# A transformer block with sliding attention: small LayerNorm operations on ScalarE, a wait for GpSimd's power, attention weights turned by VectorE

## The chip, the core and the metric

The kernel runs on one core of a Trainium2 chip. A core has five engines with their own instruction lists: TensorE (PE in the profile) multiplies matrices into PSUM, VectorE (DVE) and ScalarE (ACT) do elementwise work, GpSimd (POOL) small general work, and SyncE (SP) issues DMAs. They run side by side and wait for each other on semaphores only. The metric is the device time of one execution in microseconds. Before the change the median of three runs is 239.69 us (237.97 to 240.04).

## What is computed

One block with a residual stream `x` of 2048 positions by 512 features, in bf16. It has adaptive LayerNorm (shift, scale and gate come from a condition vector `c`), attention of 32 heads of 16 features over a window of 8 positions that lie 2 apart, and a gated feed-forward part with 1792 hidden features.

```python
mod = (silu(c) @ w_mod).reshape(1, 6, 1, -1)
sa, ca, ga, sb, cb, gb = mod[:, 0], mod[:, 1], mod[:, 2], mod[:, 3], mod[:, 4], mod[:, 5]
h = layernorm(x) * (1 + ca) + sa
# attention: H, W, dil = 32, 8, 2
idx = arange(S)[:, None] - (arange(W) * dil)[None, :]      # the 8 positions of each query
logits = einsum('bhsd,bhswd->bhsw', q, k[idx]) * 16 ** -0.5
logits = where(idx >= 0, logits, -1e9)
o = einsum('bhsw,bhswd->bhsd', softmax(logits), v[idx])
x = x + ga * (o @ wo)
h = layernorm(x) * (1 + cb) + sb
x = x + gb * ((silu(h @ w1) * (h @ w3)) @ w2)
```

## The kernel before, in words

Positions are cut into 16 tiles of 128 (`T` = 0 to 15). The program first records operations (`Program.op`, `Program.dma`), each with its engine, its function and what it reads and writes. Then `place` puts them in the order of a written-out table `ORDER`, and buffers in the slots of a table `SLOTS`. Each engine runs its operations in the order in which the table has them, and no other. `synchronize` adds the waits that follow from reads and writes and from the reuse of buffers (`o.prev`). So a list is fixed, and an engine whose next operation isn't ready stands still, even if a later one is.

The stages, and the lines that the prediction names:

- Lead: 24 warm-up matmuls on a constant (`warm`, L518), the modulation from `c` (L504), loads on SyncE (`load_x`, L413; all DMAs are issued at L124). Tiles 0 and 1 come in one load.
- First LayerNorm (`ln_stats`): VectorE statistics (L555, L556), plus epsilon (L561 on VectorE for tiles 0 and 1, L563 on GpSimd after), the power -0.5 on GpSimd (L565), then the normalisation on VectorE (L571 for tile 0, L576 for the others). `ln_T` turns the result on TensorE (L636) or by DMA, and ScalarE or VectorE scales and shifts it (L644, L651, L621).
- Projections of q, k (L691) and v (L711). v goes out to DRAM and comes back shifted (`values`), eight positions side by side on the partitions.
- `logits`: VectorE multiplies q with the eight shifted k in one operation of 4096 elements (L742, the large product `sb_pq`), and TensorE sums over each head with 32-column matmuls, four side by side (L752). For tile 0 one more matmul (L749) puts the mask in.
- `shift`, `exps`, `softmax`, always for a pair of tiles: maximum (L764), subtraction (L769), exponential on ScalarE (L782), sum (L794), reciprocal (L796), product (L797). Then `turn`: TensorE transposes the weights, four transposes of 128x128 for a pair (L807), and ScalarE copies them out of PSUM (L811).
- `values`: VectorE multiplies the shifted v with the weights (L827, 4096 elements, the value product), TensorE sums them (L855), ScalarE copies (L861), a DMA transposes, TensorE multiplies with `wo` (L867), and VectorE adds the residual (L871).
- Second LayerNorm (`ln_sums`), for a pair of tiles: mean on GpSimd (L586), squares on ScalarE (L590), variance plus epsilon (L596), power (L597) and bias (L599) on GpSimd, normalisation on ScalarE (L601).
- Feed-forward part: `ffn_unit` has two matmul groups (L883), a silu on ScalarE (L889) and a product on VectorE (L892); `ffn_w2` multiplies with w2 (L921, L909) and `store` adds the residual (L931) and writes out.

The table interleaves the feed-forward part of early tiles with the attention of later ones. `o.lock` marks operations that hold a port which VectorE and GpSimd share: by default those of GpSimd, and by hand the large VectorE operations (L576, L742, L827, the scaling of `wo` and `w2`). Before the change nothing in the program reads that mark.

Of the kernel before, what the change touches and what calls it, by code (L numbers as in the profile page):

```python
# [73 lines left out]
class Program:  # L74
# [68 lines left out]
    def place(self, order, slots):  # L143
# [129 lines left out]
def _build(p, A_x, A_wqkv, A_wo, B_w1, B_w3, B_w2, c, w_mod, out):  # L273
# [36 lines left out]
    before = sb([P, W, 2, 16], bf, "before")  # L310
# [114 lines left out]
    load_x(0, 2, 1)  # L425
# [123 lines left out]
    def ln_stats(Ts):  # L549
# [10 lines left out]
        if i < 2:  # L560
            o = p.op("dve", lambda e: e.tensor_scalar(rsn, mv[:, i:i + n, 1], EPS, None, op0=ALU.add), 65, k, r=vms, w=[va])  # L561
# [6 lines left out]
        for T in Ts:  # L568
            vn = Val("xn", xnpool)
            if T == 0:  # L570
                p.op("dve", lambda e, vn=vn, T=T: e.scalar_tensor_tensor(vn.at[:], x_sb[:, T, :], mv[:, T, 0:1], bass.AP(rs, T, [[2 * NT, P], [0, D]]),  # L571
                                                                         op0=ALU.subtract, op1=ALU.mult), 600, ("nm", T),
                     r=[vx[T], vr] + vms, w=[vn])
                vns.append(vn)
                continue
# [6 lines left out]
    def ln_sums(Ts):  # L582
# [3 lines left out]
        p.op("pool", lambda e: e.tensor_scalar(nm[:, i:i + n, 0], sx[:, i:i + n, 0], -1.0 / D, None, op0=ALU.mult), 215, k,  # L586
             r=[vsx[T] for T in Ts], w=[vnm])
        for T, vn in zip(Ts, vns):
# [7 lines left out]
        o = p.op("pool", lambda e: e.tensor_scalar(rsn, var[:, i:i + n, 0], 1.0 / D, EPS, op0=ALU.mult, op1=ALU.add), 210, k, r=vvs, w=[va])  # L596
        o = p.op("pool", lambda e: e.tensor_tensor(rsn, rsn, bass.AP(cst, 1, [[2, P], [0, n]]), ALU.pow), 600, k, r=[va, vcst],  # L597
                 w=[vr], lead=o)
        p.op("pool", lambda e: e.tensor_tensor(nb[:, i:i + n, 0], nm[:, i:i + n, 0], rsn, ALU.mult), 210, k, r=[vr, vnm], w=[vb], lead=o)  # L599
        for T, vn in zip(Ts, vns):  # L600
            p.op("act", lambda e, vn=vn, T=T: e.activation(vn.at[:], x_sb[:, T, :], ACT.Identity, bias=nb[:, T, :],  # L601
# [129 lines left out]
    def logits(Ts):  # L731

        vl = Val("ps_l", psum)
        for i, T in enumerate(Ts):
# [11 lines left out]
            def red(e, i=i, T=T, vp=vp):  # L746
                c0 = vl.at * 512 + i * W * 32
                if T == 0:
                    e.matmul(PALL[0:32, c0:c0 + W * 32], ones[:, 0:32], before[:], start=True, stop=False, tile_position=(0, 0))  # L749
                for ft in range(KT):  # L750
                    for q in range(4):
                        ins = e.matmul(PALL[32 * q:32 * q + 32, c0:c0 + W * 32], E_sb[:, ft, :], bass.AP(vp.at, ft * P + 32 * q, [[W * KT * P, P], [KT * P, W], [1, 2], [2, 16]]),  # L752
                                       start=(ft == 0 and (T > 0 or q > 0)), stop=(ft == KT - 1), tile_position=(0, 32 * q))
# [35 lines left out]
    def softmax(Ts, vl, ve, vx_):  # L789
# [7 lines left out]
        p.op("dve", lambda e: e.tensor_tensor(ve.at[0][:, 0:n], bass.AP(PALL, bank(vl).offset, [[8 * 512, P], [W * 32, n], [1, 32], [32, W]]),  # L797
# [279 lines left out]
```

## Time and profile before

| | |
|---|---|
| median of three runs (lowest, highest) | 239.69 us (237.97, 240.04) |
| span of the profiled execution | 237.7 us |
| instructions in it | 4535 |
| HBM read, written | 29.62 MB, 4.21 MB |
| GpSimd: L596, L597, L599 of the second LayerNorm, mean of eight | 766, 703, 618 ns |
| GpSimd: L563, L565 of the first, mean of seven | 207, 706 ns |
| ScalarE's L590 and L601 | 714 and 806 ns |

The profile is of one execution, and its span runs from the first to the last instruction of the core. A "busy" time is a sum over one engine. A row of the timeline has start, length, engine, line, operation, output and inputs with partitions by elements, and a count where several are merged; instructions of one engine overlap a little, so several in a row take less than the sum of their lengths. In square brackets stands how long the engine had been idle, and what ended it. A row of the waits reads: who waited, for whom, microseconds in all, how often, the longest. A row of the stretches has, for each engine, busy time and instructions in that stretch, then TensorE's granted clock, the DMA engines' busy share and the rate. "PEld" is TensorE's loading of weights, which runs beside its matmuls.

### The profile page before, as it was taken

The page shows a single profiled execution, that of the slowest core. Times are in us where ns is not written, and L with a number is a line of the kernel's source. Part 1 is how long each engine was busy: PE and PEld are TensorE (multiplying, and loading weights), DVE is VectorE, ACT ScalarE, POOL GpSimd, SP SyncE. Part 2 cuts the span into 40 slices and gives each one's busy share as a digit, 9 for nine tenths or more (in the row PEclk, how much of TensorE's full clock was granted, in tenths as well). Part 3 has the DMA queues.
Part 4 walks back from the last instruction along what each step waited for, and adds up shares of the span by engine and source line. Part 5 has one row for each costly group of instructions (what it writes and reads, how often), then busy time and mean ns, then how long its engine had stood idle before and what let it go on. Part 6 is the DMA issues. An engine that isn't in the chain of part 4 may idle for free.

```text
span 237.7 us, 4535 instructions
## 1 busy us (share of the span) xinstructions
PE 229.7 (97%) x1781; PEld 136.2 (57%) x1806; DVE 179.4 (75%) x279; ACT 138.5 (58%) x267; POOL 29.2 (12%) x66
## 2 busy tenths in 40 slices
PE   7999999999999998999999999999999999999995
PEld 4776454445588674664444444444475457485774
DVE  5699999999999989999999999682654403434433
ACT  2289577999978744985865594837473405040300
POOL 4434100013002000240002520012010000000000
PEclk9999999999999999999999999999999999999999
DMA  6999999999999999897981693642203000000202
GB/s 216 372 337 322 158 237 299 208 269 283 353 200 270 243 249 199 173 260 177 247 234 47 182 234 72 154 132 46 67 19 91 3 0 0 6 19 0 70 0 88
DMA packets 46317, 38.85 MB, mean 163 GB/s; under 512 B 21704, under 2 KB 37080, under 8 KB 46296
## 3 DMA queue, kind: packets, MB, share of 16 engines
q1 hardware_dynamic: 46288, 38.56, 66.9%
q8 instruction: 14, 0.23, 0.4%
q14 instruction: 7, 0.06, 0.1%
q10 hardware_dynamic: 8, 0.00, 0.0%
HBM read 29.62 MB, written 4.21 MB: 142 GB/s over the span
## 4 chain that ended last, share of the span: by engine, by line
PE 74%; DMA 8%; DVE 8%; SPq 4%; ACT 3%; issue 2%; ACTq 0%; DVEq 0%
PE pall L883 38%; PE pall L921 18%; DMA sb_x<-in_A_x_dram 5%; PE pall L867 5%; SPq L124 4%; PE pall L691 4%; DMA sb_vsh<-v_scratch_dram 3%; PE pall L909 3%; PE pall L855 2%; PE pall L752 2%; PE pall L711 2%; DVE sb_vsh L827 2%; DVE sb_pq L742 2%; DVE sb_hh L892 1%; ACT sb_h L621 1%
## 5 line engine op out<-in xcount | busy, mean ns | idle before, releaser
L883 PE MATMUL pall<-sb_h,sb_w 128*128 128x256 bf16 (+1 forms) x664 | 101.9, 307 | 1.8 <-DVE sb_hh L892 0.9
L883 PEld LDWEIGHTS pall<-sb_h,sb_w 128*128 128x128 bf16 x672 | 64.8, 98 | 37.2 <-issue 2.8
L889 ACT ACTIVATE sb_sg<-pall 128x256 bf16<-128x256 f32 (+1 forms) x84 | 35.6, 453 | 54.1 <-PE pall L883 53.0
L892 DVE TENSOR_TENSOR sb_hh<-sb_sg,pall 128x256 bf16<-128x256 bf16 (+1 forms) x84 | 39.9, 505 | 34.8 <-PE pall L883 32.7
L921 PE MATMUL pall<-sb_w,sb_hh 128*128 128x512 bf16 x190 | 44.0, 379 | 0.3
L742 DVE TENSOR_TENSOR sb_pq<-sb_q,sb_kT 128x4096 bf16<-128x4096 bf16 x16 | 36.3, 2282 | 0.0
L921 PEld LDWEIGHTS pall<-sb_w,sb_hh 128*128 128x128 bf16 x196 | 19.0, 98 | 21.6 <-DVE sb_hh L892 0.4
L691 PE MATMUL pall<-sb_h,sb_wqkv 128*128 128x512 bf16 (+1 forms) x154 | 30.2, 335 | 0.5 <-issue 0.2
L827 DVE TENSOR_TENSOR sb_vsh<-sb_vsh,sb_al 128x4096 bf16<-128x4096 bf16 x12 | 27.3, 2287 | 2.1 <-DMA sb_vsh<-v_scratch_dram 2.1
L621 ACT ACTIVATE sb_h<-sb_h,sb_modc 128x512 bf16<-128x512 bf16 (+1 forms) x24 | 16.5, 743 | 10.1 <-DMA sb_h<-sb_xn 10.1
L691 PEld LDWEIGHTS pall<-sb_h,sb_wqkv 128*128 128x128 bf16 x160 | 14.7, 98 | 11.8 <-ACT sb_ac L861 0.4
L931 DVE TENSOR_TENSOR sb_o<-pall,sb_x 128x512 bf16<-128x512 f32 (+1 forms) x18 | 11.1, 625 | 10.5 <-PE pall L921 6.8
L711 PE MATMUL pall<-sb_wqkv,sb_h 128*128 128x512 bf16 x62 | 15.5, 379 | 0.2
L867 PE MATMUL pall<-sb_wo,sb_ot 128*128 128x512 bf16 x61 | 15.3, 379 | 0.3 <-issue 0.2
L586 POOL TENSOR_SCALAR sb_nm<-sb_sx 128x2 f32<-128x2 f32 x8 | 1.7, 218 | 105.2 <-DVE sb_x L871 105.1
L644 ACT ACTIVATE sb_h<-pall,sb_modc 128x256 bf16<-128x256 bf16 (+1 forms) x18 | 9.9, 612 | 7.5 <-DVE sb_modc L509 6.5
L861 ACT ACTIVATE sb_ac<-pall 128x512 bf16<-128x512 f32 x16 | 9.5, 595 | 7.2 <-PE pall L855 7.1
L601 ACT ACTIVATE sb_xn<-sb_x,sb_nb,sb_rs 128x512 bf16<-128x512 bf16 x16 | 12.4, 806 | 0.7 <-POOL sb_nb L599 0.6
L871 DVE SCALAR_TENSOR_TENSOR sb_x<-pall,sb_x 128x512 bf16<-128x512 f32 x16 | 10.9, 686 | 1.5 <-PE pall L867 1.3
L590 ACT ACTIVATE sb_xn<-sb_x,sb_nm 128x512 bf16<-128x512 bf16 x16 | 11.4, 714 | 0.7 <-POOL sb_nm L586 0.7
L721 ACT ACTIVATE sb_v<-pall 128x512 bf16<-128x512 f32 x16 | 9.5, 600 | 2.8 <-PE pall L711 2.8
L555 DVE BATCH_NORM_STATS2 sb_st<-sb_x 128x6 f32<-128x512 bf16 x16 | 10.6, 680 | 0.8 <-DMA sb_x<-in_A_x_dram 0.7
(87 smaller groups left out, 208.3 us busy)
## 6 DMA issues: line engine op xcount, KB each, us to landing
sb_vsh<-v_scratch_dram SPq DMA_DIRECT2D x48, 256.0 KB, 5.5
sb_vshx<-v_scratch_dram SPq DMA_DIRECT2D x16, 256.0 KB, 4.6
sb_w<-in_B_w_dram SPq DMA_DIRECT2D x6, 512.0 KB, 7.9
sb_w<-in_B_w_dram SPq DMA_DIRECT2D x6, 384.0 KB, 5.4
v_scratch_dram<-sb_v SPq DMA_DIRECT2D x16, 128.0 KB, 6.4
out_dram<-sb_o SPq DMA_DIRECT2D x14, 128.0 KB, 1.8
sb_wqkv<-in_A_wqkv_dram SPq DMA_DIRECT2D x6, 256.0 KB, 6.3
sb_x<-in_A_x_dram SPq DMA_DIRECT2D x4, 256.0 KB, 6.4
```

The costliest lines, as they stand in the source:

```text
L590: p.op("act", lambda e, vn=vn, T=T: e.activation(vn.at[:], x_sb[:, T, :], ACT.Square, bias=nm[:, T, :], accum_out=var[:, T, :]), c_act(512 ...
L601: p.op("act", lambda e, vn=vn, T=T: e.activation(vn.at[:], x_sb[:, T, :], ACT.Identity, bias=nb[:, T, :], scale=rs[:, NT + T, :]), c_act(5 ...
L621: return e.activation(vh.at[:, ft, 0:n * P], vh.at[:, ft, 0:n * P], ACT.Identity, bias=modc[:, 8 * which + ft:8 * which + ft + 1], scale=m ...
L691: ins = e.matmul(bank(vp)[:, j * n:(j + 1) * n], wqkv[:, t, col:col + P], vh.at[:, t, 0:n], start=(t == ORDER[0] and j == 0), stop=(t == O ...
L711: ins = e.matmul(bank(vp), vh.at[:, t, tt * P:(tt + 1) * P], wqkv[:, t, 2 * D:3 * D], start=(t == ORDER[0]), stop=(t == ORDER[-1]))
L742: return e.tensor_tensor(vp.at[:], in0, in1, ALU.mult)
L827: return e.tensor_tensor(v_w, v_w, a_w, ALU.mult)
L867: ins = e.matmul(bank(vy), vt.at[:, ft, :], wo[:, ft, :], start=(ft == 0), stop=(ft == KT - 1))
L883: ins = e.matmul(bank(vp)[:, 0:n], wt[:, t, fi * P:(fi + 1) * P], vh.at[:, t, 0:n], start=(t == 0), stop=(t == KT - 1))
L889: p.op("act", lambda e: e.activation(vt.at[:, 0:n], bank(vgp)[:, 0:n], ACT.Silu), c_act(n), k, r=[vgp], w=[vt], table="silu")
L892: p.op("dve", lambda e: e.tensor_tensor(vh_.at[:, 0:n], vt.at[:, 0:n], bank(vup)[:, 0:n], ALU.mult), c_dve(n), k, r=[vt, vup], w=[vh_])
L921: ins = e.matmul(bank(vz), vhh[fi].at[:, tt * P:(tt + 1) * P], w2[:, fi, :], start=(fi == 0), stop=(fi == NF - 1))
```

## The change

1. `place` makes each marked VectorE operation wait for the last marked GpSimd operation that stands ahead of it in the table.
2. First LayerNorm: the addition of epsilon is on VectorE for all tiles (nine operations for what were two and seven), and tile 0 is normalised by the same operation as the others.
3. Second LayerNorm: mean, variance plus epsilon and bias are ScalarE activations; the bias is one for each tile where it was one for a pair. Only the power is left on GpSimd.
4. Attention weights: VectorE turns them in blocks of 32x32, two instructions for a pair, straight into the buffer that the value product reads. The TensorE transposes, their PSUM bank and ScalarE's copy go. For this a quadrant of 32 partitions of the logits holds other positions than before (four runs of 8 instead of two interleaved runs of 16), so the mask of tile 0 takes two matmuls and two selects.
5. The load of tiles 0 and 1 becomes two.
6. `ORDER` and `SLOTS` are replaced. In TensorE's list ten warm-up matmuls stand ahead of the first modulation matmul, eleven lie between real matmuls (ten of them ahead of the first logits), and three come behind the last real one; before, all 24 were ahead.

```diff
         self.order = {e: [] for e in ENGINES}
+        small = None
         self.placed = [self.ops[i] for i in order]
         for at, o in enumerate(self.placed):
...
+            if o.eng == "pool" and o.lock:
+                small = o
+            elif o.eng == "dve" and o.lock and small is not None:
+                o.prev.append(small)
...
-    before = sb([P, W, 2, 16], bf, "before")
+    before = sb([P, 2, W, 4, 8], bf, "before")
...
-    p.op("pool", lambda e: e.affine_select(out=before[:], in_=before[:], compare_op=ALU.is_ge, fill=BEFORE, base=0,
-                                           pattern=[[-DIL, W], [1, 2], [2, 16]], channel_multiplier=0), 400, k, w=[vbefore])
+    for q in range(2):
+        p.op("pool", lambda e, q=q: e.affine_select(out=before[:, q], in_=before[:, q], compare_op=ALU.is_ge, fill=BEFORE, base=8 * q,
+                                                    pattern=[[-DIL, W], [32, 4], [1, 8]], channel_multiplier=0), 400, k, w=[vbefore])
...
-    load_x(0, 2, 1)
+    load_x(0, 1, 1)
+    load_x(1, 2, 33)
...
-        if i < 2:
-            o = p.op("dve", lambda e: e.tensor_scalar(rsn, mv[:, i:i + n, 1], EPS, None, op0=ALU.add), 65, k, r=vms, w=[va])
-        else:
-            o = p.op("pool", lambda e: e.tensor_tensor(rsn, mv[:, i:i + n, 1], bass.AP(cst, 0, [[2, P], [0, n]]), ALU.add), 210, k,
-                     r=vms + [vcst], w=[va])
+        p.op("dve", lambda e: e.tensor_scalar(rsn, mv[:, i:i + n, 1], EPS, None, op0=ALU.add), 65, k, r=vms, w=[va])
...
-            if T == 0:
-                p.op("dve", lambda e, vn=vn, T=T: e.scalar_tensor_tensor(vn.at[:], x_sb[:, T, :], mv[:, T, 0:1], bass.AP(rs, T, [[2 * NT, P], [0, D]]),
-                                                                         op0=ALU.subtract, op1=ALU.mult), 600, ("nm", T),
...
-        p.op("pool", lambda e: e.tensor_scalar(nm[:, i:i + n, 0], sx[:, i:i + n, 0], -1.0 / D, None, op0=ALU.mult), 215, k,
+        p.op("act", lambda e: e.activation(nm[:, i:i + n, 0], sx[:, i:i + n, 0], ACT.Copy, scale=-1.0 / D), c_act(n), k,
              r=[vsx[T] for T in Ts], w=[vnm])
...
-        o = p.op("pool", lambda e: e.tensor_scalar(rsn, var[:, i:i + n, 0], 1.0 / D, EPS, op0=ALU.mult, op1=ALU.add), 210, k, r=vvs, w=[va])
-        o = p.op("pool", lambda e: e.tensor_tensor(rsn, rsn, bass.AP(cst, 1, [[2, P], [0, n]]), ALU.pow), 600, k, r=[va, vcst],
-                 w=[vr], lead=o)
-        p.op("pool", lambda e: e.tensor_tensor(nb[:, i:i + n, 0], nm[:, i:i + n, 0], rsn, ALU.mult), 210, k, r=[vr, vnm], w=[vb], lead=o)
+        p.op("act", lambda e: e.activation(rsn, var[:, i:i + n, 0], ACT.Identity, bias=cst[:, 0:1], scale=1.0 / D), c_act(n), k, r=vvs + [vcst], w=[va])
+        p.op("pool", lambda e: e.tensor_tensor(rsn, rsn, bass.AP(cst, 1, [[2, P], [0, n]]), ALU.pow), 600, k, r=[va, vcst], w=[vr])
         for T, vn in zip(Ts, vns):
+            vb = Val("nbias")
+            p.op("act", lambda e, T=T: e.activation(nb[:, T, :], nm[:, T, :], ACT.Copy, scale=rs[:, NT + T, :]), c_act(1), ("nm", NT + T),
+                 r=[vr, vnm], w=[vb])
...
-                        ins = e.matmul(PALL[32 * q:32 * q + 32, c0:c0 + W * 32], E_sb[:, ft, :], bass.AP(vp.at, ft * P + 32 * q, [[W * KT * P, P], [KT * P, W], [1, 2], [2, 16]]),
-                                       start=(ft == 0 and (T > 0 or q > 0)), stop=(ft == KT - 1), tile_position=(0, 32 * q))
+                        ins = e.matmul(PALL[32 * q:32 * q + 32, c0:c0 + W * 32], E_sb[:, ft, :], bass.AP(vp.at, ft * P + 8 * q, [[W * KT * P, P], [KT * P, W], [32, 4], [1, 8]]),
+                                       start=(ft == 0 and (T > 0 or q > 1)), stop=(ft == KT - 1), tile_position=(0, 32 * q))
...
-        vt, val = Val("ps_at", psum), Val("al", alpool)
+        val = Val("al", alpool)
 
         def turn(e):
-            b = bank(vt).bitcast(bf)
-            for i in range(n):
-                at = b[:, i * 256:(i + 1) * 256].rearrange("p (q y h) -> p q y h", q=4, y=2)
-                for y in range(2):
-                    ins = e.transpose(at[:, :, y, :], bass.AP(ve.at[0], i * W * 32 + y * 16 * W, [[2 * W * 32, P], [1, P]]), ident[:])
+            for y in range(2):
+                at = bass.AP(ve.at[0], W * y, [[2 * W * 32, P], [64, 4 * n], [16, 4], [1, W]])
+                ins = e.transpose(bass.AP(val.at, H * y, [[2 * 8 * H, P], [2 * H, 4 * n], [1, H]]), at)
             return ins
 
-        p.op("pe", turn, 114 * n, ("at", Ts[0]), r=[va, vident], w=[vt], hold=[ve])
-        p.op("act", lambda e: e.activation(val.at[:, 0:n].rearrange("p n g h -> p (n g h)"), bank(vt).bitcast(bf)[:, 0:2 * n * P], ACT.Copy),
-             c_act(256 * n), ("at", Ts[0]), r=[vt], w=[val])
+        p.op("dve", turn, 120 + 267 * n, ("at", Ts[0]), r=[va], w=[val], hold=[ve], lead=o, lock=False)
...
 ORDER = [
...
 SLOTS = [
...
```

More of the change, by code (lines that the diff above doesn't have):

```diff
@@ L748, in red @@
                 if T == 0:
-                    e.matmul(PALL[0:32, c0:c0 + W * 32], ones[:, 0:32], before[:], start=True, stop=False, tile_position=(0, 0))
+                    for q in range(2):
+                        e.matmul(PALL[32 * q:32 * q + 32, c0:c0 + W * 32], ones[:, 0:32], before[:, q], start=True, stop=False,
+                                 tile_position=(0, 32 * q))
                 for ft in range(KT):
                     for q in range(4):
-                        ins = e.matmul(PALL[32 * q:32 * q + 32, c0:c0 + W * 32], E_sb[:, ft, :], bass.AP(vp.at, ft * P + 32 * q, [[W * KT * P, P], [KT * P, W], [1, 2], [2, 16]]),
-                                       start=(ft == 0 and (T > 0 or q > 0)), stop=(ft == KT - 1), tile_position=(0, 32 * q))
+                        ins = e.matmul(PALL[32 * q:32 * q + 32, c0:c0 + W * 32], E_sb[:, ft, :], bass.AP(vp.at, ft * P + 8 * q, [[W * KT * P, P], [KT * P, W], [32, 4], [1, 8]]),
+                                       start=(ft == 0 and (T > 0 or q > 1)), stop=(ft == KT - 1), tile_position=(0, 32 * q))
                 return ins
```

5 lines of the change are left out of this document (1 added, 4 removed), and 133 rows, old and new, of tables (ORDER, SLOTS).

## Prediction

> **What bounds the kernel now.** I read the busy shares, then the stretches between the points where the work changes character, then the waits inside the longest of them. PE is TensorE, DVE VectorE, ACT ScalarE, POOL GpSimd.
>
> ```profile
> PE 229.7 (97%) x1781; PEld 136.2 (57%) x1806; DVE 179.4 (75%) x279; ACT 138.5 (58%) x267; POOL 29.2 (12%) x66
> ```
> ```profile
> core 0: us, PE busy (x) PEld busy (x) DVE busy (x) ACT busy (x) POOL busy (x), PEclk, DMA share, GB/s
> 12.46:22.90 10.44, 10.39 (x98) 7.20 (x96) 10.35 (x31) 9.82 (x20) 4.04 (x10) 1.00 1.10 324
> 22.90:127.70 104.80, 102.37 (x884) 59.22 (x899) 102.20 (x126) 78.07 (x150) 9.80 (x20) 1.00 1.04 233
> 127.70:160.00 32.30, 31.88 (x222) 14.89 (x217) 29.38 (x38) 21.13 (x37) 6.75 (x9) 1.00 0.60 151
> 160.00:237.70 77.70, 74.60 (x491) 47.11 (x495) 29.93 (x60) 25.92 (x58) 3.28 (x7) 1.00 0.11 31
> ```
>
> The page alone says "TensorE, 97%". The stretches say more. From 12.46 to 127.70 VectorE is as full as TensorE: in the 104.80 us from 22.90 it is idle for 104.80 - 102.20 = 2.6 us. Only after 160 does it thin out to 29.93 of 77.70. So until 127.70 two engines share the bound, and afterwards TensorE has it alone. The waits between 22.90 and 127.70 show how little either has to spare:
>
> ```profile
> DVE sb_vsh L827 <- DMA sb_vsh<-v_scratch_dram: 1.3, 2, 1.0
> DVE sb_x L871 <- PE pall L867: 0.6, 2, 0.4
> PE pall L883 <- DVE sb_hh L892: 0.9, 1, 0.9
> PE pall L855 <- DVE sb_vsh L827: 0.4, 1, 0.4
> PE pall L883 <- DVE sb_attn L797: 0.2, 1, 0.2
> ```
> ```profile
> 125.39 2.29 DVE L827 TENSOR_TENSOR sb_vshx<-sb_vshx,sb_al 128x4096 bf16<-128x4096 bf16 x1
> 126.98 0.61 PE L855 MATMUL pall<-sb_vsh,sb_ind 128*32 128x512 bf16 x8
> 127.42 1.05 PE L752 MATMUL pall<-sb_pq,sb_E 128*32 128x256 bf16 x32
> 128.33 0.61 PE L855 MATMUL pall<-sb_vshx,sb_ind 128*32 128x512 bf16 x8
> ```
>
> The last fence is the hand-over that I build the sum on. The value product of tile 10 ends on VectorE at 125.39 + 2.29 = 127.68, and TensorE, with two tiles of logits in between, sums it at 128.33. TensorE comes 0.65 us behind, so almost anything that VectorE gains in work ahead of this point moves TensorE.
>
> **The change part by part.** The attention weights first, because they put the most work on the full engine.
>
> ```profile
> 100.17 0.74 DVE L892 TENSOR_TENSOR sb_hh<-sb_sg,pall 128x256 bf16<-128x256 bf16 x2
> 107.16 0.41 DVE L892 TENSOR_TENSOR sb_hh<-sb_sg,pall 128x256 bf16<-128x256 bf16 x1
> 51.44 0.55 DVE L796 RECIPROCAL sb_ssum<-sb_ssum 128x64 f32<-128x64 f32 x1
> 52.03 0.69 DVE L797 TENSOR_TENSOR sb_attn<-pall,sb_ssum 128x512 bf16<-128x512 f32 x1
> 35.22 0.22 PE pall L807 x4
> L811 ACT ACTIVATE sb_al<-pall 128x512 bf16<-128x512 bf16 x8 | 4.8, 598 | 1.5 <-PE pall L807 1.3
> ```
>
> Removed: four transposes per pair of tiles on TensorE, 0.22 us in a row, 8 x 0.22 = 1.76 us; and eight copies of ScalarE, 4.8 us, off the path (78.07 of 104.80 busy). Added: two VectorE block transposes of 256 elements per partition for each pair. No row shows one. The nearest is L892 with 256 elements: two take 0.74 and one 0.41, so the second adds 0.33 us. Two turns are 0.66, and as they need the result of L797 I add the 0.04 that stands between the end of the reciprocal, 51.99, and 52.03: 0.70 us a pair. The low end is the rate of the all-bf16 product above, 2.29/4096 = 0.56 ns an element, for 512 elements, with twice the 0.04: about 0.4. The high end is two of L892 without overlap and the 0.04: about 0.9. I take 0.70, since L892 has the same size. In the new order list six of the eight pairs stand ahead of the product of tile 10: 6 x 0.70 = 4.2 us (2.4 to 5.4).
>
> The Trainium skill, "VectorE: DVE Perf Modes", section on the three transpose paths, has a price that no row here shows: 311 ns for a block transpose of 128x128 on VectorE. An estimate by it is 4 x 0.31 = 1.2 us a pair with nothing overlapped, and the sum below would be 3.2 us more, 245.5.
>
> First LayerNorm.
>
> ```profile
> 4.65 0.15 DVE L561 TENSOR_SCALAR sb_rs<-sb_mv 128x1 f32<-128x1 f32 x1
> 4.72 0.68 DVE L555 BATCH_NORM_STATS2 sb_st<-sb_x 128x6 f32<-128x512 bf16 x1
> 5.73 0.74 DVE L571 SCALAR_TENSOR_TENSOR sb_xn<-sb_x,sb_mv,sb_rs 128x512 bf16<-128x512 bf16 x1
> 12.46 1.29 DVE L555 BATCH_NORM_STATS2 sb_st<-sb_x 128x6 f32<-128x512 bf16 x2 [0.71 <-DMA sb_x<-in_A_x_dram]
> 0.79 0.46 SPq L124 DMA_DIRECT2D sb_x<-in_A_x_dram  x1
> ```
>
> Seven additions of epsilon move to VectorE at 4.72 - 4.65 = 0.07 us each: +0.5 (to 1.1 if none overlaps). Tile 0's normalisation gets shorter (0.74 to about 0.41), but VectorE then waits for other things in the lead; whatever it gains ends in the 0.71 us wait for the load of tiles 4 and 5, which starts the full stretch at 12.46. That wait is the cover, so I book 0. The split load adds one issue of 0.46 us on SyncE ahead of all later loads. In 12.46 to 22.90 the loads keep the DMA share at 1.10, so most of that issue hides behind data still moving: +0.3 for the lead (0.1 to 0.8).
>
> ```profile
> 3.46 3.14 PE L518 MATMUL pall<-sb_ones 128*128 128x256 bf16 x17
> 8.96 2.35 PE L691 MATMUL pall<-sb_h,sb_wqkv 128*128 128x256 bf16 x20 [0.16 <-DMA sb_wqkv<-in_A_wqkv_dram]
> ```
>
> Fourteen of the 24 warm-up matmuls leave the head of TensorE's list: three go behind the last real matmul, eleven among real work, 11 x 2.35/20 = 1.3 us. Those at the head take 3.14/17 = 0.185 us each, the same width later 0.118: with fewer of them the first twenty real matmuls may run at the slow pace, 20 x 0.067 = 1.3 us. Both lie where TensorE will be waiting for loads and for VectorE; I cost them at nothing, and at +1.3 each if that cover is gone.
>
> The second LayerNorm and the new wait.
>
> ```profile
> 50.90 0.22 POOL L586 TENSOR_SCALAR sb_nm<-sb_sx 128x2 f32<-128x2 f32 x1 [20.98 <-DVE sb_x L871]
> 53.03 0.71 POOL L597 TENSOR_TENSOR sb_rs<-sb_rs,sb_cst 128x2 f32<-128x2 f32 x1
> 53.31 2.28 DVE L742 TENSOR_TENSOR sb_pq<-sb_q,sb_kT 128x4096 bf16<-128x4096 bf16 x1
> 53.81 1.82 POOL L599 TENSOR_TENSOR sb_nb<-sb_nm,sb_rs 128x2 f32<-128x2 f32 x1
> 76.77 0.20 POOL L599 TENSOR_TENSOR sb_nb<-sb_nm,sb_rs 128x2 f32<-128x2 f32 x1
> ACT sb_xn L601 <- POOL sb_nb L599: 0.6, 1, 0.6
> L590 ACT ACTIVATION_READ_ACCUMULATOR sb_xn<-sb_x,sb_nm 128x1 f32 x16 | 3.0, 191 | 0.0
> ```
>
> L599 takes 0.20 us, and 1.82 when a 2.28 us product is running: it ends when the product does. Moving it and its kin to ScalarE takes these stalls out of GpSimd, but all that waited for them was 0.6 us of ScalarE: off the path, 0. Four small ScalarE instructions per pair come in for three on GpSimd; at the 191 ns of ScalarE's smallest row 8 x 4 x 0.19 = 6.1 us, about what the copies leave (4.8) on an engine 58% busy: 0. The power stays on GpSimd, and now every large VectorE product waits for the power that stands ahead of it in the list; behind it on VectorE are the feed-forward products that TensorE's second matmuls read. At 53.31 a product started 0.28 us into a power of 0.71 and still took 2.28: there was no cost to avoid, and with the wait that one starts 0.43 late. Four such powers and two of the first LayerNorm's late ones come before tile 10. Between the last residual and the waiting product the list has 3.8 to 5.6 us of VectorE work, the chain took 53.74 - 50.90 = 2.8 here, so most waits will be short: +0.8 (0, to 6 x 0.71 = 4.3). The skill's "SBUF — State Buffer", section on the two separate sides, states an exclusive lock in which whoever starts second fully blocks. GpSimd's rows agree with it, VectorE's row at 53.31 does not. By that rule the wait costs nothing new, and the sum would be 0.8 less, 241.5.
>
> The new list also reorders SyncE's issues, one w1 load and some value stores and loads among them, with the same bytes. I cost that at 0. The cover is small: in the full stretch VectorE already waits 1.3 us on value loads, and whatever makes these later adds to that.
>
> **The sum.** Counted in the two order lists, what VectorE does ahead of the product of tile 10 is nearly the same: 171 operations before, 184 after. The difference is six turns, seven additions, one feed-forward product and one output addition more, and two residual additions less; all four have 512 elements and nearly cancel (-0.1). So its end moves by 4.2 + 0.5 - 0.1 + 0.3 + 0.8 = +5.7, less what VectorE's own waiting gives back. Its idle time there was 2.6; the 0.6 on L867 goes, since it is later than TensorE now, and half of the 1.3 on value loads: -1.3 (0 to -2.6). That leaves +4.4.
>
> ```profile
> 188.98 6.04 PE pall L921 x28
> 228.91 6.13 PE pall L909 x56
> 235.06 0.42 DVE sb_o L931
> ```
>
> A matmul of 512 columns takes 6.04/28 = 0.216 us and one of 256 takes 6.13/56 = 0.109. TensorE's slack at the hand-over takes 0.5 of the 0.65. Behind the hand-over TensorE has two pairs of transposes (0.44) and one feed-forward half (4 x 0.216 = 0.86) less: -1.3. The tail after 235.06 stays as it is.
>
> +4.4 - 0.5 - 1.3 = +2.6 us. The profiled execution spans 237.7; the median of the three runs is 239.69 and the lowest 237.97, so this execution was near the lowest, and the table's median has 2.0 more around it. The span should be 240.3; on the median that is 239.69 + 2.6 = 242.3.
>
> **Rivals.** First, not slower: TensorE alone decides. That needs VectorE's net addition ahead of tile 10 to stay below 0.65, the slack at the hand-over. Then the transposes (-1.76) and TensorE's waits on VectorE (0.9 + 0.4 + 0.2 = 1.5) come off. Against them stand more switches into and out of the 32-column matmuls: the new list has them in 18 groups, the old one in 14.
>
> ```profile
> 84.74 0.62 PE L752 MATMUL pall<-sb_pq,sb_E 128*32 128x256 bf16 x16
> 85.72 0.94 PE L883 MATMUL pall<-sb_h,sb_w 128*128 128x256 bf16 x7
> ```
>
> That group has 16 matmuls of 256 and 8 of 512 columns, four side by side: 4 x 0.109 + 2 x 0.216 = 0.87 of the 0.98 us to the next full matmul; with as much on the way in, 0.2 a group, 0.8 for four. With three warm-ups in the full stretch (0.3): -1.76 - 1.5 + 0.8 + 0.3 = -2.2, 237.5. For it speak the 97%; against it the 2.6 us of idle VectorE time.
>
> Second, no change: the turn is at its low end (6 x 0.3 = 1.8 less) and half of what idle time I left VectorE is given back too (-0.6). +2.6 - 2.4 = +0.2, 239.9. For it speaks that TensorE's work now comes earlier against VectorE's: every residual in the new list has its output matmul several microseconds ahead. Against it, that no row shows a VectorE operation of 256 elements under 0.33.
>
> Third, slower still: the powers come late. ScalarE now carries the whole chain to them, behind evictions in its own list, and each of six products waits its full 0.71: +4.3 in place of +0.8, 245.8. It decides once the chain takes longer than the 3.8 us of VectorE work in front of the product; against it, 2.8 here.
>
> **How the numbers follow.** About 1% is what a measurement of this kernel can tell from no change: 237.3 to 242.1. The likeliest case has 0.52 and a range of its own of 240.3 to 244.5, a little over half of it above 242.1 (0.29, and 0.23 below). The first rival has 0.22; its time lies at the edge, so 0.15 of it counts as faster (TensorE's colder start is cheaper than I fear, or the lead shorter) and 0.07 as the same. The second has 0.12, all the same; the third 0.14, all slower. Together: faster 0.15, same 0.42, slower 0.43. The low bound is the sum with the turn at 0.40, no waits, 0.1 of lead and all idle time given back, 2.6 - 1.8 - 0.8 - 0.2 - 1.3 = -1.5: 238.2. The high ends added up (+1.2, +0.6, +0.5, +3.5, +1.3) would be 249.4; as they won't meet I stop a little past the third rival, at 246.0.
>
> **What would show it.** The turn as VectorE instructions of 128x256 near 0.42 us, 16 of them. VectorE idle under 2.6 us between its first large product and the product of tile 10, and that product ending near 132, while TensorE's waits name VectorE's products (L752, L855) by several microseconds in all. GpSimd's powers at 0.7 us with no long ones among them, and waits of VectorE on them of under a microsecond together. TensorE's time from the sum of tile 10 to the end 1.3 shorter than the 106.7 from 128.33 to 235.04. I am wrong if the product of tile 10 ends before 129, or if TensorE reaches its sum later than VectorE allows.

## Result and profile after

| | before | after |
|---|---|---|
| median (lowest to highest) | 239.30 us (237.97 to 240.04) | 242.73 us (241.95 to 243.21) |
| span of the profiled execution | 237.7 us | 241.4 us |

The ratio is 1.0147, interval 1.0108 to 1.0186: slower by 1.5%, little but clear of the noise. The forecast was 242.3. The median before is now that of four runs, so it lies 0.4 below the 239.69 from which the forecast started.

The busy shares of the changed kernel, and its stretches, with the same columns as the stretches before the change:

```profile
PE 229.3 (95%) x1749; PEld 133.9 (55%) x1775; DVE 183.4 (76%) x302; ACT 141.6 (59%) x291; POOL 20.2 (8%) x36
```
```profile
0.00:12.46 12.46, 7.20 (x69) 5.23 (x70) 6.52 (x27) 2.72 (x4) 5.53 (x22) 1.00 0.86 285
12.46:22.90 10.44, 10.34 (x108) 8.30 (x108) 9.86 (x34) 8.12 (x16) 3.05 (x5) 1.00 1.11 311
22.82:132.64 109.82, 106.83 (x904) 59.43 (x915) 106.85 (x141) 81.77 (x164) 6.76 (x6) 1.00 0.92 222
```

VectorE's full stretch runs from its first large product to the end of the value product of tile 10. It was 104.8 us long with 2.6 idle; now it is 109.82 with 109.82 - 106.85 = 2.97 idle. GpSimd fell from 29.2 us to 20.2, as meant. The timeline around the hand-over:

```profile
126.76 0.76 DVE L805 STREAM_TRANSPOSE sb_al<-sb_attn 128x256 bf16<-128x256 bf16 x2
130.36 2.28 DVE L823 TENSOR_TENSOR sb_vsh<-sb_vsh,sb_al 128x4096 bf16<-128x4096 bf16 x1
131.24 0.61 PE L851 MATMUL pall<-sb_vsh,sb_ind 128*32 128x512 bf16 x8
132.79 0.61 PE L851 MATMUL pall<-sb_vsh,sb_ind 128*32 128x512 bf16 x8
```

A turn of a pair takes 0.76 us. The product of tile 10 ends at 130.36 + 2.28 = 132.64, 4.96 later than before, and TensorE's sum starts 0.15 behind it, where it was 0.65. Up to here it looks like the prediction. The waits of the two engines between 22.9 and 133 do not:

```profile
DVE sb_vshx L823 <- DMA sb_vshx<-v_scratch_dram: 0.6, 1, 0.6
DVE sb_mx L764 <- PE pall L752: 0.6, 1, 0.6
DVE sb_x L867 <- PE pall L863: 0.6, 2, 0.4
DVE sb_vsh L823 <- DMA sb_vsh<-v_scratch_dram: 0.5, 1, 0.5
PE pall L863 <- DMA sb_ot<-sb_ac: 1.4, 2, 0.9
PEld pall L851 <- DVE sb_vsh L823: 0.8, 2, 0.4
```

These are the long ones, in us in total, times and longest. If VectorE held TensorE, its value products would stand in TensorE's waits with several microseconds. They stand there only at the weight loads (PEld), with 0.8 us. The lead comes next: its stretch in the kernel before, and TensorE's timeline, first of the kernel before, then of the changed one.

```profile
0.00:12.46 12.46, 10.47 (x102) 7.75 (x104) 7.57 (x28) 3.56 (x6) 5.32 (x22) 1.00 0.89 296
```
```profile
6.76 0.55 PE L504 MATMUL pall<-sb_csT_bf,sb_wm_s 128*128 128x1 bf16 x16
8.19 0.61 PE L691 MATMUL pall<-sb_h,sb_wqkv 128*128 128x256 bf16 x4
```
```profile
3.47 1.25 PE L525 MATMUL pall<-sb_ones 128*128 128x256 bf16 x5
7.87 0.56 PE L511 MATMUL pall<-sb_csT_bf,sb_wm_s 128*128 128x1 bf16 x16 [3.15 <-DMA sb_wm_s<-in_w_mod_dram]
10.38 1.06 PE L689 MATMUL pall<-sb_h,sb_wqkv 128*128 128x256 bf16 x4
11.23 0.41 PE L525 MATMUL pall<-sb_ones 128*128 128x256 bf16 x1
11.81 1.69 PE L689 MATMUL pall<-sb_h,sb_wqkv 128*128 128x256 bf16 x12
```

The modulation starts 1.1 us later, the query and key matmuls 2.2 us later, and the first four of them take (11.23 - 10.38)/4 = 0.21 us each instead of 0.118. TensorE is busy for 229.3 us in all, against 229.7 before, so the longer span is idle time of TensorE, and most of it lies here: up to 12.46 it is idle for 12.46 - 7.20 = 5.26 us, before for 1.99. (In the kernel before, the warm-up matmuls that were moved filled part of this time, so the difference alone is no price.) So two explanations stood against each other: VectorE's turn, or the lead with TensorE's own list.

### The profile page after: what moved, and what is told of

It reads as the page before. It is cut to its first block, busy times and chain, and to the rows that moved or that the text cites. A ratio compares the mean times of both kernels' runs of the same rounds, so it can differ in the third digit from the quotient of the medians.

```text
span 241.4 us, 4490 instructions
## 1 busy us (share of the span) xinstructions
PE 229.3 (95%) x1749; PEld 133.9 (55%) x1775; DVE 183.4 (76%) x302; ACT 141.6 (59%) x291; POOL 20.2 (8%) x36
## 4 chain that ended last, share of the span: by engine, by line
PE 72%; ACT 11%; DMA 9%; DVE 2%; issue 2%; SPq 1%; POOL 1%; DVEq 0%
PE pall L879 36%; PE pall L917 13%; PE pall L689 6%; PE pall L863 5%; DMA sb_h<-sb_xn 3%; DMA sb_ot<-sb_ac 3%; PE pall L851 3%; PE pall L905 3%; DMA sb_wm_s<-in_w_mod_dram 2%; ACT sb_h L619 2%; PE pall L709 2%; PE pall L752 2%; SPq L124 1%; ACT sb_xn L599 1%; POOL sb_rs L594 1%
## 5 line engine op out<-in xcount | busy, mean ns | idle before, releaser
L689 PE MATMUL pall<-sb_h,sb_wqkv 128*128 128x512 bf16 (+1 forms) x156 | 31.2, 340 | 0.8 <-ACT sb_gb_bc L554 0.2
L594 POOL TENSOR_TENSOR sb_rs<-sb_rs,sb_cst 128x2 f32<-128x2 f32 x8 | 8.0, 996 | 153.8 <-ACT sb_rs L593 153.8
L927 DVE TENSOR_TENSOR sb_o<-pall,sb_x 128x512 bf16<-128x512 f32 (+1 forms) x18 | 11.1, 627 | 12.5 <-PE pall L917 8.1
L823 DVE TENSOR_TENSOR sb_vshx<-sb_vshx,sb_al 128x4096 bf16<-128x4096 bf16 x4 | 9.1, 2285 | 4.6 <-DMA sb_vshx<-v_scratch_dram 4.6
L863 PEld LDWEIGHTS pall<-sb_wo,sb_ot 128*128 128x128 bf16 x64 | 6.1, 98 | 8.5 <-issue 1.4
```

The lines of the kernel that those rows point to most:

```text
L689: ins = e.matmul(bank(vp)[:, j * n:(j + 1) * n], wqkv[:, t, col:col + P], vh.at[:, t, 0:n], start=(t == ORDER[0] and j == 0), stop=(t == O ...
L823: return e.tensor_tensor(v_w, v_w, a_w, ALU.mult)
L863: ins = e.matmul(bank(vy), vt.at[:, ft, :], wo[:, ft, :], start=(ft == 0), stop=(ft == KT - 1))
```

## The experiments

Each was timed in five rounds beside the kernel before, whose median was 239.33 us in the first four, 239.38 in the next four, 239.07 in the next three and 238.60 in the last. The table puts all of them together; its three last columns are of the one profiled execution of each. "Later" is the start of the same TensorE step against the kernel whose list it has (the changed one for the upper half, the one before for the lower): first query/key matmul, sum of tile 10, and last matmul that isn't a warm-up.

| kernel | median us | ratio to before | later: q/k | sum of 10 | last |
|---|---|---|---|---|---|
| changed kernel, against before | 242.73 | 1.0147 [1.0108, 1.0186] | +2.2 | +4.5 | +3.9 |
| e1 turn left out | 243.42 | 1.0167 [1.0123, 1.0210] | -0.2 | +0.8 | +0.8 |
| e2 turn twice | 245.14 | 1.0240 [1.0200, 1.0279] | +0.3 | +2.5 | +2.4 |
| e3 no wait for the power | 243.02 | 1.0165 [1.0126, 1.0204] | +0.2 | +0.2 | +0.5 |
| e4 turn on TensorE | 254.36 | 1.0643 [1.0586, 1.0701] | | | |
| e5 one load | 242.81 | 1.0142 [1.0111, 1.0173] | -1.0 | -0.3 | -0.1 |
| e6 warm-ups first | 243.06 | 1.0155 [1.0118, 1.0193] | -0.3 | +1.0 | +0.7 |
| e7 both of these | 242.39 | 1.0132 [1.0101, 1.0163] | -1.1 | -0.2 | -0.6 |
| e10 lead, and turn left out | 242.68 | 1.0153 [1.0116, 1.0189] | -1.0 | +0.1 | 0.0 |
| e8 before, turn on VectorE | 240.92 | 1.0071 [1.0044, 1.0097] | +0.1 | +2.1 | +2.1 |
| e11 before, new lead | 243.43 | 1.0176 [1.0139, 1.0213] | +1.7 | +3.3 | +3.8 |
| e12 before, second LayerNorm on ScalarE | 249.70 | 1.0481 [1.0438, 1.0524] | +0.6 | +5.9 | +7.9 |
| e9 before, all edits but the list and lead | 253.94 | 1.0623 [1.0587, 1.0660] | +0.5 | +10.1 | +14.8 |

### The turn in the new list: left out, doubled

```diff
-                at = bass.AP(ve.at[0], W * y, [[2 * W * 32, P], [64, 4 * n], [16, 4], [1, W]])
-                ins = e.transpose(bass.AP(val.at, H * y, [[2 * 8 * H, P], [2 * H, 4 * n], [1, H]]), at)
+                at = bass.AP(ve.at[0], W * y, [[2 * W * 32, P], [64, 1], [16, 4], [1, W]])
+                ins = e.transpose(bass.AP(val.at, H * y, [[2 * 8 * H, P], [2 * H, 1], [1, H]]), at)
```

This is e1, whose buffers GpSimd fills with zeros ahead of their first use. For e2, in the changed kernel's loop:

```diff
+                e.transpose(bass.AP(twin[Ts[0] // 2 % 4], H * y, [[2 * 8 * H, P], [2 * H, 4 * n], [1, H]]), at)
                 ins = e.transpose(bass.AP(val.at, H * y, [[2 * 8 * H, P], [2 * H, 4 * n], [1, H]]), at)
```

> The changed kernel with only the first 32x32 blocks of each pair's weights turned (one tile's first group), so most weights the value products read are zeros: the turn's 0.75 us a pair become about 0.1, nothing else moves. Theory (VectorE's added work ahead of the product of tile 10 is the cost): that product ends 3.5 to 4 us earlier, about 129 in place of 132.6, and the time falls from 242.7 by 2.5 to 4 us, to 238.7 to 240.2. Rival A (the later loads and the cold start in the lead are the cost): the time stays, 242 to 243.5, with TensorE's sum of tile 10 near 132.8 as now. Rival C (TensorE's own list, with more groups of 32-column matmuls and warm-ups among real work): also 242 to 243.5.

> The changed kernel with every turn issued twice, the second copy into a buffer that nobody reads: 0.70 to 0.75 us more of VectorE a pair, six pairs ahead of the product of tile 10. Theory: that product ends 4.2 to 4.5 us later, the time is 242.7 + 4 = 246.7 (245.7 to 247.5). Rival C (TensorE is the bound by itself): less than 1.5 us more, under 244.2. Rival A: at most 1 us more, as VectorE has 8.8 us idle from its first instruction to there.

Without the turn nothing is won: 243.42. My theory falls in its plain form. The waits of e1's VectorE and TensorE between 22.9 and 133, VectorE's stretch to the end of the product of tile 10, its product of tile 4, and the hand-over:

```profile
DVE sb_vsh L828 <- DMA sb_vsh<-v_scratch_dram: 3.2, 2, 2.0
DVE sb_vshx L828 <- DMA sb_vshx<-v_scratch_dram: 0.6, 1, 0.6
PE pall L856 <- DVE sb_vsh L828: 1.8, 2, 1.3
```
```profile
22.82:133.24 110.42, 107.89 (x907) 59.30 (x909) 105.06 (x143) 81.85 (x165) 6.75 (x6) 1.00 0.91 220
```
```profile
82.15 2.29 DVE L828 TENSOR_TENSOR sb_vsh<-sb_vsh,sb_al 128x4096 bf16<-128x4096 bf16 x1 [1.98 <-DMA sb_vsh<-v_scratch_dram]
130.95 2.29 DVE L828 TENSOR_TENSOR sb_vsh<-sb_vsh,sb_al 128x4096 bf16<-128x4096 bf16 x1
133.62 0.61 PE L856 MATMUL pall<-sb_vsh,sb_ind 128*32 128x512 bf16 x8
```

VectorE has 106.85 - 105.06 = 1.8 us less to do, and its waits on the value loads grow from 0.6 + 0.5 to 3.8 us. The product of tile 10 ends at 133.24, later than with the turn. What VectorE won it spent waiting for value loads, which do not come earlier because VectorE is faster, and TensorE, which never waited for a value product at its matmuls in the changed kernel, now waits 1.8 us for two of them. One load makes most of the difference: the last of the four for tile 4 was issued at 72.90 and landed at 82.03, where in the changed kernel it was issued at 73.00 and landed at 80.31. Up to the sum of tile 3 TensorE was 0.1 us ahead of the changed kernel, from the sum of tile 4 on it was behind it, first by 1.4. With an earlier landing the gain here would still have been small, since VectorE was ready only 80.66 - 80.17 = 0.5 us sooner. Doubling the turn costs 2.4 of the 4.2 to 4.5 us of added work, against the 4 I expected and the rivals' 1 to 1.5 at most: about 2 us of VectorE work have room in this list. (The small turns take about 0.19 us each, not the 0.05 I had assumed, so e1 takes away less than planned.)

### The wait for the power

```diff
-            if o.eng == "pool" and o.lock:
-                small = o
-            elif o.eng == "dve" and o.lock and small is not None:
-                o.prev.append(small)
```

> The changed kernel without the wait of large VectorE products for the power ahead of them in the list. Theory (the wait was nearly free: the trace shows no idle VectorE put down to a power after the lead): 242.7, between 241.9 and 243.0. Rival B (the wait is the cost, and appears as something else): 239.5 to 240.5.

243.02, a hair above what the theory allowed and nowhere near the rival: no cost of the wait and no saving by it can be told from the noise. The trace of e3 is of use for the lead, which it has in common with the changed kernel. The fast pace of its matmuls came later, at 14.09, so that the 25th query and key matmul was 1.3 us later; at the sum of tile 10 only 0.15 of that was left.

### The turn back on TensorE

```diff
-        p.op("dve", turn, 120 + 267 * n, ("at", Ts[0]), r=[va], w=[val], hold=[ve], lead=o, lock=False)
+        p.op("pe", turn, 114 * n, ("at", Ts[0]), r=[va, vident], w=[vt], hold=[ve])
+        p.op("act", lambda e: e.activation(val.at[:, 0:n].rearrange("p n g h -> p (n g h)"), bank(vt).bitcast(bf)[:, 0:2 * n * P], ACT.Copy),
+             c_act(256 * n), ("at", Ts[0]), r=[vt], w=[val])
```

(With it the old layout of the logits and the old mask.)

> The changed kernel's order of everything else, with the turn put back on TensorE (four transposes a pair) and its copy on ScalarE. Theory: VectorE has 4.5 us less ahead of the product of tile 10, TensorE 1.76 us more in all: 239.5 to 240.7, at best as the kernel before. Rival A (lead and order): 242 to 243.5, and with TensorE's transposes added up to 244.

254.36, which fits neither. The four transposes and ScalarE's copy went into places that I chose by hand, and VectorE then waited for the copy:

```profile
DVE sb_vsh L824 <- ACT sb_al L808: 4.9, 1, 4.9
```

It shows the places, not the turn, and nothing else is drawn from it.

### The lead in the new list

e5 makes the first load one again. e6 moves the fourteen warm-up matmuls that follow the first modulation matmul ahead of it. e7 does both.

```diff
-    load_x(0, 1, 1)
-    load_x(1, 2, 33)
+    load_x(0, 2, 1)
```

> The changed kernel with tiles 0 and 1 in one load again, so that SyncE's list has one issue less ahead of the first modulation weights. New theory (TensorE is the bound all through; at 22.9 us it is 1.8 us of useful work behind the kernel before, because the modulation weights land 1.0 us later, nine warm-up matmuls run among the first real ones, and these run at the cold pace): the weights land near 6.9 in place of 7.7 and the time falls by 0.5 to 1.2 us, to 241.5 to 242.3. Old theory (VectorE's turn): 242.3 to 243.

> The changed kernel with all 24 warm-up matmuls ahead of the first modulation matmul, where TensorE waits for the load, as in the kernel before. New theory: 1.0 to 1.3 us of warm-ups and about 1 us of cold pace leave TensorE's list: 240.5 to 241.7, the first query and key matmuls at 0.12 us each in place of 0.21. Old theory: 242.3 to 243.

> Both of these: one load of tiles 0 and 1, and all warm-ups first. New theory: TensorE gains 2 to 3 us in the lead; VectorE, which has about 1.8 us of margin (from the run with the turn issued twice, 4.2 us more work for 2.4 us), then becomes the later one: 240.0 to 241.3. Old theory: 242.3 to 243.

None gives what the new theory wanted. In e5 the weights land at 6.53, even before the 6.9 that I expected, and TensorE starts 1.0 us earlier; as the slow pace lasts until 11.94, 0.2 of that is left at the 25th query and key matmul and 0.3 at the sum of tile 10. In e6 the pace stays slow although all warm-ups are ahead: 18 matmuls at 3.70/18 = 0.21 us. Only e7 brings a better lead, 1.7 us at the 25th query and key matmul; 0.2 of it is left at the sum of tile 10 and 0.6 at the end. TensorE's timeline in e6 and in e7, and e7's waits between 22.9 and 133:

```profile
10.11 3.70 PE L689 MATMUL pall<-sb_h,sb_wqkv 128*128 128x256 bf16 x18
```
```profile
9.30 2.61 PE L688 MATMUL pall<-sb_h,sb_wqkv 128*128 128x256 bf16 x18 [0.33 <-DVE sb_h L648]
```
```profile
DVE sb_vsh L822 <- DMA sb_vsh<-v_scratch_dram: 1.6, 2, 1.4
DVE sb_vshx L822 <- DMA sb_vshx<-v_scratch_dram: 0.8, 1, 0.8
PE pall L850 <- DVE sb_vsh L822: 1.2, 3, 0.6
```

Now TensorE waits for value products (1.2 us, none before), and VectorE for value loads (2.4 us, 1.1 before). Over e7, e5, the changed kernel and e3 the 25th query and key matmul moves by 3.0 us, and the sum of tile 10 by 0.4 (e6, nearly level at the 25th, is 1.0 later there). By these rows three chains lie close together in the new list, TensorE's list, VectorE's list and the value loads: where one was eased, a wait on another grew.

### One part of the change alone, in the old list

The old list is the better place to price a part, since the order does not change with it. e8 has the turn alone (part 4 of the change, at the places of TensorE's transposes), e11 the lead alone.

> The kernel before with one part of the change alone: the weights turned by VectorE, lead and order of the old list kept. If VectorE's added work ahead of the product of tile 10 costs by itself: 0.75 us x 6 = 4.5 later there, less the 0.65 of slack and TensorE's 1.3 behind it: 241.5 to 242.5. If TensorE alone decides, its 1.76 us of transposes come off: 237.5 to 239.3.

The hand-over in e8, and TensorE's wait on value products between 22.9 and 242:

```profile
127.47 2.29 DVE L826 TENSOR_TENSOR sb_vshx<-sb_vshx,sb_al 128x4096 bf16<-128x4096 bf16 x1
130.41 0.61 PE L854 MATMUL pall<-sb_vshx,sb_ind 128*32 128x512 bf16 x8 [0.82 <-DVE sb_hh L891]
```
```profile
PE pall L854 <- DVE sb_vsh L826: 1.7, 4, 0.7
```

Here the theory's mechanism is plain: the product of tile 10 ends at 129.76, 2.1 us later than before, TensorE stands 0.82 us before its sum until VectorE is through, and the 2.1 us stay to the last matmul. (The bracket names the operation that stands behind the product on VectorE.) The time is 240.92, below the 241.5 to 242.5 of the theory and above the rival's 239.3: +1.5 us. (The profiled execution, 241.49, is the longest of its six, so the trace shows somewhat more.) VectorE's stretch in e8:

```profile
22.90:129.76 106.86, 102.84 (x881) 57.90 (x892) 105.45 (x138) 76.20 (x145) 8.31 (x20) 1.00 1.02 229
```

e11 splits the first load of the kernel before and spreads its warm-ups as the changed kernel does:

```diff
-    load_x(0, 2, 1)
+    load_x(0, 1, 1)
+    load_x(1, 2, 33)
```

> The kernel before with the changed kernel's lead alone: tiles 0 and 1 in two loads, and of the 24 warm-up matmuls ten at the head, eleven among the real matmuls and three at the end, after as many other steps of TensorE as in the changed list. Theory: TensorE starts its query and key matmuls some 2 us later and at the cold pace: 240.3 to 241.8. Rival (the lead is covered, as booked in the prediction): 239.1 to 239.9.

```profile
7.81 0.58 PE L505 MATMUL pall<-sb_csT_bf,sb_wm_s 128*128 128x1 bf16 x16 [0.75 <-DMA sb_wm_s<-in_w_mod_dram]
9.91 1.06 PE L692 MATMUL pall<-sb_h,sb_wqkv 128*128 128x256 bf16 x4
11.62 2.72 PE L692 MATMUL pall<-sb_h,sb_wqkv 128*128 128x256 bf16 x14
131.62 0.61 PE L856 MATMUL pall<-sb_vshx,sb_ind 128*32 128x512 bf16 x8
```
```profile
PE pall L519 <- ACT sb_kT L702: 0.9, 1, 0.9
```

This is three times the cost of the turn: 243.43, +4.4 us, more than the whole change. The modulation starts 1.05 us late, the 25th query and key matmul 3.6, the first logits 3.9, the sum of tile 2 4.8, the sum of tile 10 3.3 and the last matmul 3.8. So the old list does not take the delay back. (The wait in the last row, at 56.85, is one of a warm-up that I placed on a bank still in use, and belongs to this run alone; the delay of 4.8 has it in it. Later on the delay falls to 3.3; how much of that is still the warm-up's was not separated, nor were the later loads from the moved warm-ups.)

### The second LayerNorm, and everything in the old list

e9 has every edit of the change except the split load; all its warm-ups are first, and each operation stands where its forerunner stood in the old list. e12 has these lines alone, with the epsilon and the bias moved likewise:

```diff
-        p.op("pool", lambda e: e.tensor_scalar(nm[:, i:i + n, 0], sx[:, i:i + n, 0], -1.0 / D, None, op0=ALU.mult), 215, k,
+        p.op("act", lambda e: e.activation(nm[:, i:i + n, 0], sx[:, i:i + n, 0], ACT.Copy, scale=-1.0 / D), c_act(n), k,
```

> The kernel before, its own list and lead (one load of tiles 0 and 1, all warm-ups first), with every other edit of the change: turn on VectorE, epsilon on VectorE, second LayerNorm's small operations on ScalarE, the wait for the power. Theory (two limits nearly equal, TensorE and VectorE; the turn is 1.5 us of the 3.4, the new list with its lead the rest): 240.9 to 241.7, the turn's 240.9 and up to 0.8 for epsilon and waits. Rival (the LayerNorm edits and the wait are the rest): 242.3 to 243.2.

> The kernel before, its own list, with the second LayerNorm's small operations moved to ScalarE at the places where GpSimd had them, and nothing else of the change. In the run with all edits in the old list ScalarE stood 4.45 us before one negated mean, waiting for the residual, with evictions behind it. Theory (a small operation moved to an engine that others read from puts its wait into that engine's list, and the old list has no room for it): 244 to 254, most of that run's 14.9. Rival (that run's loss is from the wait for the power, the epsilons or their meeting with the turn): 238.5 to 240.5.

With all edits but the new list and lead, the kernel takes 253.94 us, 14.9 more. e12, the second LayerNorm alone, takes 249.70 (247.28 to 251.68), 11.1 more. Its trace is of the 247.28, which alone of the six had a granted clock of 1.00 (the others 0.986 to 0.993), so the trace accounts for 8.7 us. The waits of ScalarE and TensorE in e12, TensorE's timeline, and the rows of two of its costliest steps:

```profile
ACT sb_nm L586 <- DVE sb_x L872: 8.5, 3, 3.9
PE pall L884 <- ACT sb_h L622: 3.5, 1, 3.5
```
```profile
118.95 5.99 PE L884 MATMUL pall<-sb_h,sb_w 128*128 128x512 bf16 x27 [3.50 <-ACT sb_h L622]
```
```profile
107.73 0.29 ACT L596 ACTIVATE sb_rs<-sb_var,sb_cst 128x2 f32<-128x2 f32 x1
108.10 2.22 POOL L597 TENSOR_TENSOR sb_rs<-sb_rs,sb_cst 128x2 f32<-128x2 f32 x1 [4.76 <-ACT sb_rs L596]
110.35 0.30 ACT L600 ACTIVATE sb_nb<-sb_nm,sb_rs 128x1 f32<-128x1 f32 x1 [2.33 <-POOL sb_rs L597]
163.44 0.20 ACT L586 ACTIVATE sb_nm<-sb_sx 128x2 f32<-128x2 f32 x1 [3.87 <-DVE sb_x L872]
164.19 1.90 PE L884 MATMUL pall<-sb_h,sb_w 128*128 128x512 bf16 x8 [1.51 <-ACT sb_sg L890]
```

Two things happen. The negated mean takes 0.2 us, but in ScalarE's list it stands waiting for the residual, and what stands behind it waits too: at 163.44 it has waited 3.87, and TensorE then waits 1.51 for the silu behind it. And a moved operation comes later than on GpSimd, behind ScalarE's other work: the variance plus epsilon of the pair starts at 107.73 (the last square, its input, ended at 104.48), the power after it runs beside a large product and takes 2.22 in place of 0.69, the bias waits for it, and behind normalisation and a DMA TensorE waits 3.50. On GpSimd little else stood in the list than this chain itself.

In the new list ScalarE still waits, in smaller pieces:

```profile
ACT sb_nm L583 <- DVE sb_x L867: 4.9, 5, 2.2
```

So the new list keeps the change's price down: with it, and with a lead that is worse, the same edits take 242.73 in place of 253.94.

### Both suspects off together

> The changed kernel with both suspects off together: one load of tiles 0 and 1 with seven warm-ups and then seventeen ahead of the first modulation matmul, and only the first 32x32 blocks turned (one tile's first group of each pair; most weights that the value products read are zeros). Theory (each of two limits holds the time when the other is eased, so that either alone gave nothing): 239.7 to 241.2. Rival (neither; the new list itself, with its groups of 32-column matmuls and its waits on loads, holds the time): 242 to 243.

242.68, the rival's number, but not a clean test: in its profiled execution the modulation weights landed at 7.53, where the other kernels with one load had 6.53 to 7.10, and of a lead 1.2 us better at the 25th query and key matmul 0.3 was left at the first logits. VectorE waited 2.9 us on value loads. Whether a kernel with lead, turn and value loads all eased would be faster stays open, and so does the rival, since the new list was not timed without the other edits.

## Why the prediction was right, and where not

The number was right within 0.4 us and the sign too; the reason was half of the story, and part of the closeness was luck. I forecast +2.6 and measured 242.73 - 239.30 = +3.4; the base of 239.69 was 0.4 too high, and 0.8 of error in the change became 0.4 in the time. (I had also read the span of 237.7 as that of one of the shortest executions. A time lies 1.7 to 1.8 us above its span, 243.20 against 241.4 in the changed kernel, so it was an ordinary one; the sum does not rest on it.)

- **The turn.** 0.76 us a pair against 0.70, and six of them 4.2 us from start to start, as booked: right. The estimate worked out from the Trainium skill ("VectorE: DVE Perf Modes", the three transpose paths), 1.2 us a pair, is not borne out; the trace decides. In the old list the prediction's own terms for the turn alone, 4.2 - 1.3 - 0.5 - 0.44 = 2.0, meet the measured 2.1 at the last matmul, but not one by one: VectorE's busy time grew by 105.45 - 102.20 = 3.25, its idle time gave back 1.2, the 0.65 between product and sum stayed, and nothing came off behind the hand-over.
- **The sum to the hand-over.** VectorE +4.96 against +4.4, TensorE's sum +4.46 against +3.9. The terms: work in VectorE's stretch 106.85 - 102.2 = +4.65, as much as listed (4.2 + 0.5 - 0.1), though not item by item; no delay from the lead instead of +0.3; no wait for the power seen instead of +0.8; idle time given back -1.3, and measured +0.4, since the value loads still cost 1.1 of 1.3, the residual's 0.6 stayed and 0.6 on logits (L764) came. The errors cancel in part.
- **The lead: the step that failed.** I booked +0.3 for the later loads and "at nothing, and at +1.3 each if that cover is gone" for the interior warm-ups and the cold pace. For VectorE the cover was there (first large product at 22.82, before 22.89). For TensorE in the old list it was not: e11 has 1.05 of later loads and 3.6 in all at the 25th matmul, near 1.05 + 1.3 + 1.3 as priced (by then seven warm-ups had taken 1.3, and some fifteen matmuls had run at 0.213 in place of 0.109, 1.6), and 3.8 at the end. TensorE was at 97%; a cover that I had argued from waits in the lead was not a cover for the engine that ends last. In the new list most of such a delay is taken back by tile 10 (e3, e7), as VectorE and the value loads come no earlier.
- **What sets the end.** "VectorE's added work moves the hand-over" is shown for the old list (e8) and not for the new one: e1 takes the turn out and wins nothing. In the new list the lead, VectorE's work and the value loads seem to hold about the same time, which is read from the waits and was not shown by a run that eases all three. The turn alone (+1.5) and the lead alone (+4.4) come to more than the whole 3.4 in the old list, so the new one gives something back; how the 3.4 divide in it was not settled.
- **The second LayerNorm** was costed at 0 since ScalarE is 58% busy. In the new list no run contradicts that; in the old one it costs 9 to 11 us (e12). Busy time was the wrong measure; what counts is what stands ahead of a moved operation and behind it while it waits.
- **The rivals.** TensorE alone (237.5) left the lead out of its sum. No change (239.9) and late powers (245.8) did not come; for the powers, e3 moves nothing that can be told from the noise.
- **Signposts.** 16 turns near 0.42 us: yes. VectorE idle under 2.6: no, 2.97. TensorE's waits naming value products by several microseconds: no, and this was the sign that the reason was incomplete. The product of tile 10 near 132: yes, 132.64. Powers all at 0.7: no, two of the 17 took 2.99 and 2.81 (at 33.30 and 137.84), each beside a large product, and ended 0.55 us after it. VectorE's waits on powers under 1 us together: no, 1.4, though all ahead of the first large product. The rest of TensorE after the sum of tile 10 1.3 shorter: 0.6 by the last matmul.

## What to carry to other kernels

Where two engines are full, do not price a change by the one whose list it lengthens alone: take the lag of the same instruction against the kernel before at three or four points, and see where it arises and whether anything takes it back. A delay of the fullest engine in the first microseconds was still there at the end of the old list (3.6 us at the 25th matmul, 3.8 at the last), while in the new one 1.3 us were all but gone by tile 10. A small operation moved to an engine costs what stands behind it in that engine's list while it waits, and what its own followers lose while it stands behind others, not its own 0.2 us, so edit and order have to be priced together. If taking a cost away wins nothing, look which wait has grown by the same amount before saying that the cost was free.

## What the hardware showed unexpectedly

The split of the first load delays the next one by more than the issue. The modulation weights were issued about 0.4 us later (1.72 against 1.31 in the changed kernel and the one before), but landed 1.0 later: at 7.5 to 8.0 in all seven traces with two loads, at 6.5 to 7.1 in six of seven with one, and at 7.53 in the seventh (e10).

TensorE's slow pace does not show in the granted clock: the row for 0.00 to 12.46 says 1.00, as does every stretch of the lead, while matmuls of 256 columns start 0.21 us apart until 11.45 in the changed kernel, 12.86 in e6 and 13.74 in e11, and 0.109 afterwards. The moment differs between executions with the same lead: 11.6 in the changed kernel, 12.5 in e1, 13.2 in e2 and 14.1 in e3. The Trainium skill ("TensorE: Matmul & The Clock Gate", the HAM clock gate) says that the pace doubles after some 3.4 us of sustained activity, counted in a free-running window. By these traces it came 2.4 us after TensorE's last pause of 0.4 us or more in the kernel before, 3.6 in the changed kernel and 5.9 in e3 and e11, so the rule agrees in kind, with a wide spread. Warm-up matmuls right ahead of the real work do not make sure of the pace: in e6 all of them ran at the slow pace, a pause of 0.41 us followed, and the slow pace went on for 4.7 us more, while in e10, after as slow a row of warm-ups and a pause of 0.37 us, the query and key matmuls ran at the fast pace from the first on. Whether the length of the pause decides that was not tested.
